# Channel attention and an ELU feed-forward layer on one core: the idle products behind the last real ones

## The chip, the cores and the metric

The kernel runs on one core of a Trainium2 chip. The metric is the device time of one execution in microseconds, given as the median of several runs.

## The reference

Attention over channels, followed by a two-layer network with an ELU between its layers:

```python
# q, k, v: (4, 6080, 256) float32; w_in: (256, 2048), w_out: (2048, 256) float64
qn = q / (np.linalg.norm(q, axis=1, keepdims=True) + 1e-06)
kn = k / (np.linalg.norm(k, axis=1, keepdims=True) + 1e-06)
s = kn.transpose(0, 2, 1) @ qn / tau            # (4, 256, 256)
a = softmax(s)                                  # exp(s - max), over the sum + 1e-9
x = (v @ a).astype(np.float32).reshape(24320, 256)
h = x @ w_in                                    # (24320, 2048)
g = np.where(h > 0.0, h, np.exp(np.minimum(h, 0.0)) - 1.0)
return (g @ w_out).astype(np.float32)
```

## The kernel before

The four batches are taken one after the other. For each, the kernel forms the 256 x 256 matrix of products of k and q ("gram"), makes the softmax of it, and multiplies it into the first weights, so that `v @ a @ w_in` becomes `v @ wp` with a `wp` for each batch. These weights lie in the tiles `wps[b]`, one for each of two halves of the channels (`KT` = 2).

The bulk of the time goes into the feed-forward part. The 6080 tokens of a batch are cut into 12 chunks, eight of 512 tokens and four of 496, 48 chunks in all. For each chunk and each of 16 blocks of 128 hidden features there is one step of the main loop: `h_item` makes the hidden values `ph` with six products (L323 to L325), `elu` and `split_g` make the activations `g` from them on ScalarE and VectorE, and `out_item` multiplies them with `w_out` in six products (L361, L363, L365) into `po`. Every number is split into a high and a low part of type float32r, and three products of parts make one of full width: that is why there are three lines. `out_item` for a step stands three steps (`LAG`) behind its `h_item`. The tile `wo` holds the high and low parts of all of `w_out` as (128 partitions, 16 blocks, 2 parts, 256 columns), in one contiguous piece for each partition.

PSUM has 8 buffers: two for the gram matrices, three (`WB`, tag `w`) that `ph` and other short-lived results take in turn, and three for `po`. The order of instructions on each engine follows the order of the program, with the work of the next batch strewn between the steps. Some other products run as full float32 rather than float32r: the product of the softmax with the first weights of batch 0 (L281) and batch 0's gram matrix (L446). L166 is a gram product of the later batches, whose moving operand is two blocks of 256 columns.

The end of the kernel: after the last `out_item` the function `store` copies the last two blocks of `po` to SBUF (L387, L381, L382) and stores them (L389, L383 from SyncE's queue, L384 from ScalarE's). Behind the main loop, at the end of the program, stand twelve more products on TensorE whose result, the tile `pd`, nobody reads (L696 to L702):

- three (L696) with weights from `wp` and a moving operand of 496 columns from `vt`, the last chunk of v;
- three (L698) with the moving operand replaced by one column repeated 496 times, and weights from `wo`, `wp`, `wo`;
- three (L700) with both operands read as bfloat16;
- three (L702) with only 64 of the 128 rows.

All twelve write into one `pd`, a buffer of the ring of three.

Of the kernel before, what the change touches and what calls it, by code (L numbers as in the profile page):

```python
# [7 lines left out]
F32 = mybir.dt.float32  # L8
F32R = mybir.dt.float32r
U32 = mybir.dt.uint32  # L10
BF16 = mybir.dt.bfloat16
AF = mybir.ActivationFunctionType
ALU = mybir.AluOpType
AX = mybir.AxisListType
# [15 lines left out]
def channel_attention_then_elu_ffn(ctx: ExitStack, tc, q, k, vT, tau, w_in, w_out, outT):  # L30
# [8 lines left out]
    nc = tc.nc  # L39
    B, N, C = q.shape  # L40
# [3 lines left out]
    P = 128  # L44
    KT = C // P
    FT = F // P
    DT = D // P
    CH = 512
    sizes = chunk_sizes(N, CH)
    NB = len(sizes)  # L50
    NCH = B * NB
# [7 lines left out]
    WB = 3  # L59
# [9 lines left out]
    ps = ctx.enter_context(tc.tile_pool(name="ps", bufs=4, space=bass.MemoryType.PSUM))  # L69
# [9 lines left out]
    wo = const.tile([P, FT, 2, D], F32R, name="wo")  # L79
# [213 lines left out]
    def span(c):  # L293

        b, x = divmod(c, NB)
        return b, b * N + sum(sizes[:x]), sizes[x]
# [17 lines left out]
    wps = {}  # L314
# [126 lines left out]
    wi64, wo64, vraw, vts = {}, {}, {}, {}  # L441
# [156 lines left out]
    for c in range(NCH - 1):  # L598
# [6 lines left out]
        x, y = ((1, 2), (4, 6), (17, 19))[c] if c < M - 1 else (c * FT + 9, c * FT + 12)  # L605
# [6 lines left out]
    for b in range(1, B):  # L612
# [31 lines left out]
        for g in range(g0, NG):  # L644
            x = s0 + length * (g - g0) // (NG - g0)
# [5 lines left out]
        x = s1 - FT - 6  # L651
# [12 lines left out]
    for i in range(len(steps) + LAG):  # L664
        if i < len(steps):
            c, f = steps[i]
# [5 lines left out]
        if j >= 0:  # L672
            c, f = steps[j]
# [14 lines left out]

    c, n = NCH - 1, span(NCH - 1)[2]
    pd = ps.tile([P, CH], F32, tag="w", bufs=WB, name="pd")
    hi, lo = (vts[c][:, 0, x, 0:n] for x in range(2))
    wide, narrow = wps[B - 1][0][:, 0, 0:P], wo[:, 0, 0, 0:P]
    for _ in range(3):
        nc.tensor.matmul(pd[:, 0:n], wide, hi, start=True, stop=True)  # L696
    for w in (narrow, wide, narrow):
        nc.tensor.matmul(pd[:, 0:n], w, vts[c][:, 0, 0, 0:1].to_broadcast([P, n]), start=True, stop=True)  # L698
    for w, m in ((wide, hi), (narrow, lo), (wide, hi)):
        nc.tensor.matmul(pd[:, 0:n], w.bitcast(BF16)[:, 0:P], m.bitcast(BF16)[:, 0:n], start=True, stop=True)  # L700
    for w, m in ((wide, hi), (narrow, lo), (wide, hi)):
        nc.tensor.matmul(pd[:, 0:n], w[0 : P // 2], m[0 : P // 2], start=True, stop=True)  # L702


# [29 lines left out]
```

## Time and profile before

| | before |
|---|---|
| median of 3 runs | 2291.22 us (2289.93 to 2294.47) |
| profiled execution: time | 2289.16 us |
| profiled execution: span from first to last instruction | 2287.4 us |
| TensorE busy | 2283.2 us (100%), 10244 products |
| VectorE busy | 1533.4 us (67%) |
| ScalarE busy | 1480.7 us (65%) |
| mean granted TensorE clock | 1.000 |

The time of a run is some 1.8 us longer than the span, which counts from the first to the last instruction of the profiled execution. In the rows below, a line of the order of instructions gives the start in us from the span's start, the duration in us, the engine, the line of the kernel, the operation, what it writes and reads, and how many alike follow one another. PE is TensorE's products, PEld its loads of weights, DVE is VectorE, ACT is ScalarE, SP is SyncE; a q behind an engine's name is its queue. Products are pipelined: the duration of one (0.38 us) is longer than the step from one start to the next.

### The profile page before, as it was taken

The page shows a single profiled execution, that of the slowest core. Times are in us where ns is not written, and L with a number is a line of the kernel's source. Part 1 is how long each engine was busy: PE and PEld are TensorE (multiplying, and loading weights), DVE is VectorE, ACT ScalarE, POOL GpSimd, SP SyncE. Part 2 cuts the span into 40 slices and gives each one's busy share as a digit, 9 for nine tenths or more (in the row PEclk, how much of TensorE's full clock was granted, in tenths as well). Part 3 has the DMA queues.
Part 4 walks back from the last instruction along what each step waited for, and adds up shares of the span by engine and source line. Part 5 has one row for each costly group of instructions (what it writes and reads, how often), then busy time and mean ns, then how long its engine had stood idle before and what let it go on. Part 6 is the DMA issues. An engine that isn't in the chain of part 4 may idle for free.

```text
span 2287.4 us, 27142 instructions
## 1 busy us (share of the span) xinstructions
PE 2283.2 (100%) x10244; PEld 1900.3 (83%) x10244; DVE 1533.4 (67%) x2395; ACT 1480.7 (65%) x2425; POOL 3.2 (0%) x11
## 2 busy tenths in 40 slices
PE   9999999999999999999999999999999999999999
PEld 8778888888888888888888888888888888888888
DVE  6995766666666666666666667666666666666665
ACT  5876666666666666666666666666666666666665
POOL 0000000000000000000000000000000000000000
DMA  9220111110201111111111111121102000000000
GB/s 356 83 74 19 61 59 65 55 53 37 65 28 56 47 53 49 55 55 44 37 55 37 46 47 56 47 64 46 47 34 64 20 19 28 28 19 10 19 9 19
DMA packets 61092, 118.15 MB, mean 52 GB/s; under 512 B 6048, under 2 KB 15904, under 8 KB 60960
## 3 DMA queue, kind: packets, MB, share of 16 engines
q1 hardware_dynamic: 60816, 116.29, 15.0%
q8 instruction: 80, 1.31, 0.2%
q14 instruction: 52, 0.43, 0.1%
q10 hardware_dynamic: 144, 0.13, 0.0%
HBM read 89.39 MB, written 27.00 MB: 51 GB/s over the span
## 4 chain that ended last, share of the span: by engine, by line
PE 97%; DMA 1%; DVE 1%; ACT 0%; issue 0%; SPq 0%; DVEq 0%; ACTq 0%
PE ph L323 15%; PE po L365 15%; PE po L361 15%; PE po L363 15%; PE ph L325 15%; PE ph L324 15%; PE gram L166 3%; PE gram L169 1%; DMA room<-in_k_dram 1%; PE pw L281 1%; PE pw L284 0%; PE pw L285 0%; PE pw L283 0%; DVE acc L145 0%; DMA wi<-in_moe_w_in_dram 0%; DMA raw<-in_k_dram 0%
## 5 line engine op out<-in xcount | busy, mean ns | idle before, releaser
L82 ACT CAST g<-e 128x512 fp32r<-128x512 f32 (+1 forms) x768 | 472.4, 615 | 507.6 <-DVE e L340 275.2
L83 DVE TENSOR_TENSOR g<-e,g 128x512 fp32r<-128x512 f32 (+1 forms) x768 | 526.4, 685 | 349.4 <-ACT g L82 314.1
L361 PE MATMUL po<-g,wo 128*128 128x512 f32 (+1 forms) x1536 | 596.0, 388 | 0.3 <-ACT g L82 0.3
L365 PE MATMUL po<-g,wo 128*128 128x512 f32 (+1 forms) x1536 | 596.0, 388 | 0.0
L363 PE MATMUL po<-g,wo 128*128 128x512 f32 (+1 forms) x1536 | 595.4, 388 | 0.0
L323 PE MATMUL ph<-vt,wp 128*128 128x512 f32 (+1 forms) x1472 | 573.6, 390 | 0.0
L325 PE MATMUL ph<-vt,wp 128*128 128x512 f32 (+1 forms) x1472 | 570.7, 388 | 0.0
L324 PE MATMUL ph<-vt,wp 128*128 128x512 f32 (+1 forms) x1472 | 569.6, 387 | 0.0
L336 DVE SCALAR_TENSOR_TENSOR e<-e,ph 128x512 f32<-128x512 f32 (+1 forms) x416 | 283.6, 682 | 297.2 <-ACT e L335 296.4
L334 ACT ACTIVATE e<-ph 128x512 f32<-128x512 f32 (+1 forms) x416 | 247.1, 594 | 159.2 <-PE ph L325 155.7
L361 PEld LDWEIGHTS po<-g,wo 128*128 128x128 f32 x1536 | 288.4, 188 | 58.3 <-ACT g L82 0.7
L363 PEld LDWEIGHTS po<-g,wo 128*128 128x128 f32 x1536 | 288.4, 188 | 57.7
L365 PEld LDWEIGHTS po<-g,wo 128*128 128x128 f32 x1536 | 288.3, 188 | 52.3 <-DVE g L83 0.4
L323 PEld LDWEIGHTS ph<-vt,wp 128*128 128x128 f32 x1472 | 276.2, 188 | 56.6 <-PE po L365 0.6
L325 PEld LDWEIGHTS ph<-vt,wp 128*128 128x128 f32 x1472 | 276.3, 188 | 56.3
L324 PEld LDWEIGHTS ph<-vt,wp 128*128 128x128 f32 x1472 | 276.4, 188 | 56.0 <-issue 0.7
L335 ACT ACTIVATE e<-e 128x512 f32<-128x512 f32 (+1 forms) x416 | 261.2, 628 | 12.1
L338 ACT ACTIVATE e<-ph 128x512 f32<-128x512 f32 (+1 forms) x352 | 208.7, 593 | 79.2 <-PE ph L325 64.7
L340 DVE TENSOR_TENSOR e<-ph,e 128x512 f32<-128x512 f32 (+1 forms) x352 | 241.1, 685 | 10.7
L339 DVE TENSOR_SCALAR e<-e 128x512 f32<-128x512 f32 (+1 forms) x352 | 148.9, 423 | 49.7 <-ACT e L338 49.6
L145 DVE TENSOR_TENSOR acc<-acc,sq 128x1024 f32<-128x1024 f32 x84 | 102.6, 1221 | 12.1 <-ACT sq L144 11.4
L166 PE MATMUL gram<-qk 128*128 128x512 f32 x276 | 108.5, 393 | 0.0
(126 smaller groups left out, 1173.4 us busy)
## 6 DMA issues: line engine op xcount, KB each, us to landing
raw<-in_q_dram SPq DMA_DIRECT2D x73, 256.0 KB, 2.7
raw<-in_k_dram SPq DMA_DIRECT2D x73, 256.0 KB, 2.9
v<-in_v_dram SPq DMA_DIRECT2D x32, 512.0 KB, 3.4
out_dram<-o SPq DMA_DIRECT2D x56, 256.0 KB, 2.0
v<-in_v_dram SPq DMA_DIRECT2D x16, 496.0 KB, 3.5
out_dram<-o SPq DMA_DIRECT2D x31, 248.0 KB, 2.1
wraw<-w_scr SPq DMA_DIRECT2D x12, 512.0 KB, 3.1
room<-in_q_dram SPq DMA_DIRECT2D x16, 256.0 KB, 5.2
```

The costliest lines, as they stand in the source:

```text
L82: nc.scalar.copy(hi, src)
L83: nc.vector.tensor_sub(lo, src, hi.bitcast(F32))
L323: nc.tensor.matmul(ph[:, 0:n], wp[kt][:, 0, fs], hi, start=(kt == 0), stop=False)
L324: nc.tensor.matmul(ph[:, 0:n], wp[kt][:, 0, fs], lo, start=False, stop=False)
L325: nc.tensor.matmul(ph[:, 0:n], wp[kt][:, 1, fs], hi, start=False, stop=(kt == KT - 1))
L334: nc.scalar.activation(ev, pv, AF.Relu, scale=-1.0)
L335: x = nc.scalar.activation(ev, ev, AF.Exp, scale=-1.0)
L336: y = nc.vector.scalar_tensor_tensor(ev, ev, -1.0, pv, op0=ALU.add, op1=ALU.max)
L340: y = nc.vector.tensor_tensor(ev, pv, ev, op=ALU.max)
L361: nc.tensor.matmul(o, wo[:, f, 0, ds], hi, start=first(c, f), stop=False)
L363: nc.tensor.matmul(o, wo[:, f, 1, ds], hi, start=False, stop=False)
L365: nc.tensor.matmul(o, wo[:, f, 0, ds], lo, start=False, stop=last(c, f))
```

## The change

The twelve idle products go, and 39 others take their place, in ten groups. Each has a `pd` tile of its own from the ring of three PSUM buffers. The moving operand now comes from `wo`, seen as one flat row (`flat`) for each partition; `run(first, n)` is a piece of `n` words that starts `first` words into one of four blocks of 1024, a different one for each product of a group. The weights (`some`) are in turn four blocks of 128 columns of the last batch's `wp`. The groups:

1. four products over 512 words in order;
2. four with weights that are one column repeated 128 times;
3. four over 448 words in place of 512;
4. four that start 4 words later;
5. four that start 16 words later;
6. four that start 32 words later;
7. four that take words from the two halves of the piece in alternation (0, 256, 1, 257, ...);
8. four that take blocks of 16 words from the two halves in alternation;
9. four that take all even words and then all odd ones;
10. three over 512 words in order, with weights from `wo`.

```diff
-    c, n = NCH - 1, span(NCH - 1)[2]
-    pd = ps.tile([P, CH], F32, tag="w", bufs=WB, name="pd")
-    hi, lo = (vts[c][:, 0, x, 0:n] for x in range(2))
-    wide, narrow = wps[B - 1][0][:, 0, 0:P], wo[:, 0, 0, 0:P]
-    for _ in range(3):
-        nc.tensor.matmul(pd[:, 0:n], wide, hi, start=True, stop=True)
-    for w in (narrow, wide, narrow):
-        nc.tensor.matmul(pd[:, 0:n], w, vts[c][:, 0, 0, 0:1].to_broadcast([P, n]), start=True, stop=True)
-    for w, m in ((wide, hi), (narrow, lo), (wide, hi)):
-        nc.tensor.matmul(pd[:, 0:n], w.bitcast(BF16)[:, 0:P], m.bitcast(BF16)[:, 0:n], start=True, stop=True)
-    for w, m in ((wide, hi), (narrow, lo), (wide, hi)):
-        nc.tensor.matmul(pd[:, 0:n], w[0 : P // 2], m[0 : P // 2], start=True, stop=True)
+    flat = wo.rearrange("p f x d -> p (f x d)")
+    left = [wps[B - 1][kt][:, 0, x : x + P] for kt in range(KT) for x in (0, P)]
+
+    def probe(count, weights, moving):
+        for x in range(count):
+            pd = ps.tile([P, CH], F32, tag="w", bufs=WB, name="pd")
+            m = moving(x)
+            out = pd[:, 0 : m.free_size()]
+            if len(m.shape) == 3:
+                out = out.rearrange("p (a b) -> p a b", b=m.shape[2])
+            if len(m.shape) == 4:
+                out = out.rearrange("p (a b c) -> p a b c", b=m.shape[2], c=m.shape[3])
+            nc.tensor.matmul(out, weights(x), m, start=True, stop=True)
+
+    def some(x):
+        return left[x % 4]
+
+    def run(first, n=CH):
+        return lambda x: flat[:, x % 4 * 2 * CH + first : x % 4 * 2 * CH + first + n]
+
+    probe(4, some, run(0))
+    probe(4, lambda x: wps[B - 1][0][:, 0, x : x + 1].to_broadcast([P, P]), run(0))
+    probe(4, some, run(0, 448))
+    probe(4, some, run(4))
+    probe(4, some, run(16))
+    probe(4, some, run(32))
+    probe(4, some, lambda x: run(0)(x).rearrange("p (a b) -> p b a", a=2))
+    probe(4, some, lambda x: run(0)(x).rearrange("p (a b c) -> p b a c", a=2, c=16))
+    probe(4, some, lambda x: run(0)(x).rearrange("p (a b) -> p b a", b=2))
+    probe(3, lambda x: flat[:, 4096 + x * P : 4096 + x * P + P], run(0))
```

More of the change, by code (lines that the diff above doesn't have):

```diff
@@ L10 @@
 U32 = mybir.dt.uint32
-BF16 = mybir.dt.bfloat16
 AF = mybir.ActivationFunctionType
```

## The prediction

> **What bounds the kernel now.** I read the page first (span, busy time, chain), then the order of instructions over the last 8 us, then what the end of the program waits for, and last the spacing of products of 512 columns elsewhere in the span. From the page, the span, TensorE's busy time and the chain that ended last:
>
> ```profile
> span 2287.4 us, 27142 instructions
> PE 2283.2 (100%) x10244; PEld 1900.3 (83%) x10244; DVE 1533.4 (67%) x2395; ACT 1480.7 (65%) x2425; POOL 3.2 (0%) x11
> PE 97%; DMA 1%; DVE 1%; ACT 0%; issue 0%; SPq 0%; DVEq 0%; ACTq 0%
> ```
>
> TensorE is busy for all but 4.2 us of the span, and 97% of the chain is its own. So a product that is added behind the last one lengthens the program by its step, start to start, unless something else ends later. What stands there is in the order of instructions of the last stretch (start, duration, engine, line):
>
> ```profile
> 2282.18 0.38 PE L361 MATMUL po<-g,wo 128*128 128x496 f32 x1
> ...
> 2283.04 0.57 ACT L387 COPY o<-po 128x496 f32<-128x496 f32 x1 [2.04 <-PE po L365]
> ...
> 2283.28 0.38 PE L365 MATMUL po<-g,wo 128*128 128x496 f32 x1
> ...
> 2283.50 0.82 PE L696 MATMUL pd<-vt,wp 128*128 128x496 f32 x3
> ...
> 2283.94 0.19 PEld L698 LDWEIGHTS pd<-vt,wo 128*128 128x128 f32 x1
> ...
> 2284.16 0.37 PE L698 MATMUL pd<-vt,wo 128*128 128x496 f32 x1
> ...
> 2284.37 0.38 PE L698 MATMUL pd<-vt,wp 128*128 128x496 f32 x1
> ...
> 2284.55 0.38 ACTq L384 DMA_DIRECT2D out_dram<-o  x1
> 2284.58 0.37 PE L698 MATMUL pd<-vt,wo 128*128 128x496 f32 x1
> ...
> 2285.23 0.37 PE L700 MATMUL pd<-vt,wp 128*128 128x496 bf16 x1
> 2285.53 0.18 PEld L702 LDWEIGHTS pd<-vt,wp 64*128 64x128 f32 x1 [0.41 <-issue]
> 2285.53 0.49 PE L702 MATMUL pd<-vt,wp 64*128 64x496 f32 x1
> ...
> 2286.08 0.39 PE L702 MATMUL pd<-vt,wp 64*128 64x496 f32 x1
> ```
>
> The last real product starts at 2283.28. The twelve idle ones follow without a gap, from 2283.50 to the last start at 2286.08, and that one ends at 2286.47. Beside them run the last copies and the last store of the output (issued at 2284.55). How long the stores take, and what the program's end (SyncE, at the line that closes the kernel) waits for, stand in the answer on the output's DMAs and in SyncE's waits; the chain's last four pieces follow:
>
> ```profile
> DMA to landing us min/median/max: 1.8/1.9/2.0
> SPq L729 <- DMA out_dram<-o: 1.8, 1, 1.8
> SPq L729 <- PEq L729: 0.6, 2, 0.4
> 2283.66 0.66 PE pd L696 x3
> 2284.32 0.63 PE pd L698 x3
> 2284.95 0.64 PE pd L700 x3
> 2285.60 0.87 PE pd L702 x3
> ```
>
> The last store lands at 2284.55 + 1.8 to 2.0 = 2286.35 to 2286.55, the last product ends at 2286.47: the two tie within 0.1 us, and the chain gives the end to the products. From 2286.47 to 2287.4 there are 0.9 us of closing work, which stay as they are. So the idle products cost next to nothing today, since they lie beside the last copies and stores. That cover is used up: each microsecond more of them is a microsecond more of the program. Nothing on the other engines is late.
>
> **The change part by part.** *Removed*: the twelve products, 2286.08 − 2283.50 = 2.58 us from first start to last start. *Added*: 39 products at the same place in program order. 35 have 512 columns and four have 448, all of float32r words, each with its own weight load. Nothing moves on DVE, ACT or a DMA queue; no vector or scalar instruction reads the results, so no wait is added elsewhere.
>
> The step of an ordinary product comes from two stretches. The first is a steady run of 512 columns (24 products between the two rows); the second is one with 496 columns, above. The third pair of rows is of a product whose 512 columns lie in two separate blocks of 256, with the product behind it:
>
> ```profile
> 2084.62 0.39 PE L361 MATMUL po<-g,wo 128*128 128x512 f32 x1
> ...
> 2089.83 0.39 PE L325 MATMUL ph<-vt,wp 128*128 128x512 f32 x1
> ...
> 401.96 0.40 PE L166 MATMUL gram<-qk 128*128 128x512 f32 x1
> 402.19 0.39 PE L361 MATMUL po<-g,wo 128*128 128x512 f32 x1
> ...
> 140.35 1.72 PE pw L281 x4
> ```
>
> Between the first two rows lie 23 steps: 5.21 / 23 = 0.2265 us for 512 columns in order. For 496 it is (2283.28 − 2282.18) / 5 = 0.220. Both are 0.443 ns a column. The product with a jump after 256 columns takes 0.23, so one jump costs nothing visible. The products of L698, whose moving operand is one column repeated 496 times, take 0.21 (2284.16, 2284.37, 2284.58), or 0.42 ns a column. The difference of 0.02 ns is about a twentieth of a column. I read it as the price of walking: roughly one column's time for each 16 columns (64 bytes) that an ordinary walk passes, and none where the walk stays on one word. That is an estimate from these rows, and no row shows a walk that jumps with every column. The upper row for one is L281, the full float32 products, which run as two instructions each: 1.72 / 4 = 0.43 us for 512 columns, double time.
>
> Group by group, in the order of the diff:
> 1. Four in order, 512 columns: 4 × 0.2265 = 0.91.
> 2. Four with one weight column repeated 128 times. The load of weights takes 0.19 (L698's row) beside the product ahead of it, under the step of 0.2265, so I take 0.91. If such a load took double (0.38) it would stick out by 0.15, 0.6 in all; if repeating saves load time, nothing is won, since it is hidden.
> 3. Four of 448 columns: 448 × 0.443 ns = 0.198, together 0.79.
> 4. to 6. Twelve that begin 4, 16 or 32 words later. By the reading above a late start touches at most one stretch more, one column in 512. 12 × 0.2265 = 2.72.
> 7. Four that alternate between two halves 256 words apart, column by column. Bounds: 0.2265 if the walk is free, and 0.86 (a whole L281 product, two instructions) if it is worse than double. I take 0.43, one column's time for each new place, which is also L281's figure for one instruction: 1.72.
> 8. Four that alternate between the halves in blocks of 16 words. The number of 64-byte stretches is that of an ordinary walk, and a jump between blocks cost nothing in L166: 0.91.
> 9. Four that take every second word and then the others. They pass 64 stretches where an ordinary walk passes 32, so 0.0135 us more each: 0.24, together 0.96. The bounds are 0.2265 and 0.43.
> 10. Three in order with weights from the other array: 0.68.
>
> The sum is 0.91 + 0.91 + 0.79 + 2.72 + 1.72 + 0.91 + 0.96 + 0.68 = 9.60 us. Less the last step, the last start lies 9.37 us behind 2283.50, at 2292.87, and it ends 0.39 later as today. The change is 9.37 − 2.58 = +6.8 us. The profiled execution would come to a span of 2294.2 and a time of 2289.16 + 6.8 = 2296.0. The median of the runs shown, 2291.22, lies 2.06 above that execution; on it, 2298.0.
>
> For groups 7 and 9 there is a rule in the Trainium skill, "SBUF — State Buffer", section "SBUF: two separate sides": the memory is read in lines of 16 bytes, two hits on a line are needed to hide its access, and each access that crosses to a new line pays. By it group 7 (one word per line) pays and group 9 (two words per line) does not: 9.54 in place of 9.60. No row here shows either walk.
>
> A further item is where the results go. Each new product writes a tile of its own, in the ring of three PSUM buffers that the real `ph` products used, where the twelve shared one tile. The writer before it in a buffer is again TensorE, three products earlier, and ends 0.39 after its start, while the next user starts 3 × 0.2265 = 0.68 after it. I cost it at nothing.
>
> **The rivals.** *Cheap walks* (the change does little that a walk can feel). If groups 7 and 9 go at 0.2265 like L166's, the sum is 35 × 0.2265 + 0.79 = 8.72, and the change 8.72 − 0.23 − 2.58 = +5.9: 2297.1. If all go at L698's 0.21, 0.42 ns a column, it is about +5.4: 2296.6. For it speaks L166; against it, that L698 shows a walk does have a price.
>
> *Dear walks.* If a column from a new place costs as much as a whole L281 product, group 7 takes 4 × 0.86 = 3.44, and if group 9 takes 0.43, 1.72: the sum rises by 2.48, the change to +9.3, 2300.5. Nothing in the profile speaks for it but the absence of such a row.
>
> *Waits on the ring of buffers.* If each product from the fourth on waits until TensorE has reported the one three earlier, the load of weights starts late. The nearest row for a step whose weight load was not ahead is the change from L700 to L702: 0.30 in place of 0.22, so 36 × 0.08 = 2.9 more: +9.7, 2300.9. Against it: 0.39 is less than 0.68, and real `ph` products go round the same ring at 0.22.
>
> *Placed ahead.* The new operands (`wo`, the last `wp`) are ready long before the end, so the products could be put among the last real ones. TensorE has no idle time there to take them, and then the last copies and stores, 2286.55 − 2283.28 = 3.3 us from the last real start, would follow all 39: last real start 2283.28 + 9.6, landing 3.3 later, against 2286.47 today, +9.7: 2300.9. Against it: the operands of the twelve (`vt`, `wp`, `wo`) were also ready by then, and they ran behind L365.
>
> *Not slower.* The products have no reader. If the build dropped them, the end would belong to the last store at 2286.35 to 2286.55, a change of −0.1 to +0.1: 2291.2. It decides only if none of the 39 is in the trace. Against it: the twelve have no reader either and all twelve are there.
>
> **How the numbers follow.** The difference that a measurement can tell from none is about 0.2%, 4.6 us. The forecast has 0.62, cheap walks 0.22, dear walks 0.07, ring waits 0.04, placed ahead 0.03, dropped 0.02. All but the last are over 4.6 us. But the three runs shown lie between 1.3 below their median and 3.3 above it, and medians of two kernels can differ by 1 to 2 us: I give one in ten of the forecast (6.8, a margin of 2.2) and a quarter of the cheap walks (a margin of 0.8 to 1.3) to a difference within 0.2%: 0.06 + 0.06, and with the dropped case about 0.13. Faster by over 0.2% has no mechanism; 0.02 for what I have not thought of. Slower is 0.85. The range goes from cheap walks less the runs' spread, 2296.6 − 2.1 = 2294.5, to the dear ones with some spread, 2301.5.
>
> **What would show it right or wrong.** The real products should end as today, the last L365 starting near 2283.3, and DVE and ACT should have the same instruction counts. TensorE's count should rise by 27 to 10271. In the tail, groups 1, 2, 4 to 6, 8 and 10 should step at 0.2265, group 3 at 0.198, group 9 near 0.24 and group 7 near 0.43; the last product should end 6.8 us later, the last store landing where it does now, and SyncE's last wait should be for TensorE alone. It is wrong if the 39 stand ahead of the last L365, if a wait appears within them, if group 7 steps at 0.23 or at over 0.5, or if the stretch before 2283 changes length.

## The result and the profile after

| | before | after |
|---|---|---|
| median | 2292.26 us (2289.93 to 2294.47, 5 runs) | 2298.68 us (2297.58 to 2302.35, 5 runs) |
| profiled execution: time, span | 2289.16, 2287.4 us | 2298.68, 2296.9 us |
| last real product starts | 2283.28 us | 2285.86 us |
| first to last start of the idle products | 2.58 us (12) | 9.54 us (39) |

The ratio of after to before is 1.003, with a 95% interval of 1.0016 to 1.0045. The kernel became slower by 6.4 us at the medians, 0.28%. The page of after, its span, busy times and chain:

```profile
span 2296.9 us, 27196 instructions
PE 2291.4 (100%) x10271; PEld 1907.1 (83%) x10271; DVE 1533.3 (67%) x2395; ACT 1479.8 (64%) x2425; POOL 3.1 (0%) x11
PE 97%; DMA 1%; DVE 1%; ACT 0%; issue 0%; SPq 0%; ACTq 0%; DVEq 0%
```

TensorE has 27 products more; VectorE and ScalarE have the same counts. The order of instructions at the end of after, and then what SyncE waited for there (the lines of the kernel are one lower than before, L364 is L365):

```profile
2285.86 0.38 PE L364 MATMUL po<-g,wo 128*128 128x496 f32 x1
...
2286.08 9.23 PE L702 MATMUL pd<-wo,wp 128*128 128x512 f32 x36
...
2287.13 0.37 ACTq L383 DMA_DIRECT2D out_dram<-o  x1
...
2295.14 0.88 PE L702 MATMUL pd<-wo 128*128 128x512 f32 x3
```
```profile
SPq L746 <- PE pd L702: 7.0, 1, 7.0
SPq L746 <- DMA out_dram<-o: 1.8, 1, 1.8
```

All 39 idle products stand behind the last real one, without a gap. The last store is issued at 2287.13 and waited for 1.8 us; after that SyncE waits another 7.0 us for TensorE alone. Before, the two ended within 0.1 us of each other.

The span grew by 9.5 us, more than the tail: 6.95 us (9.535 − 2.583, unrounded) are the idle products, and 2.6 us were lost before the last real product. Busy time in two stretches of the start (length, then TensorE's busy time and products, weight loads, DVE, ACT, POOL, granted clock, DMA), first of before, then of after:

```profile
40.00:50.00 10.00, 9.40 (x48) 8.05 (x47) 8.11 (x11) 6.03 (x8) 0.00 (x0) 1.00 1.05 410
50.00:60.00 10.00, 9.90 (x48) 8.34 (x47) 7.84 (x23) 4.63 (x13) 0.00 (x0) 1.00 0.45 176
```
```profile
40.00:50.00 10.00, 7.45 (x38) 6.30 (x37) 9.01 (x10) 5.83 (x7) 0.00 (x0) 1.00 1.04 402
50.00:60.00 10.00, 10.00 (x44) 8.54 (x44) 5.93 (x21) 3.99 (x11) 0.00 (x0) 0.83 0.63 244
```

The idle time is one wait of TensorE, for VectorE's sum of the squares of the first batch (again before, then after):

```profile
PE pn L185 <- DVE acc L182: 0.6, 1, 0.6
```
```profile
PE pn L184 <- DVE acc L181: 2.5, 1, 2.5
```

After, TensorE idles 2.55 us where before it idled 0.60, and then it has a granted clock of 0.83 on average over 10 us. All this is in the first batch, 2.2 ms ahead of the change. Every other kernel profiled has the long wait, 2.3 to 3.2 us, and the one execution of before is alone with 0.6. The start varies between executions: the last real product starts at 2284.27 in a kernel with no idle products at all (below), and between 2285.16 and 2288.59 in five others that differ only in their tails. So the medians, and the tails by themselves, carry the comparison, not the two profiled spans.

The steps by group follow, as stretches from the first start of each group to the first start of the next, TensorE alone (length, busy time, products that lie at least in part in the stretch, clock, DMA); the last is that of two steps:

```profile
2286.08:2286.99 0.91, 0.91 (x5) 1.00 0.00 0
2286.99:2287.92 0.93, 0.93 (x5) 1.00 0.94 351
2287.92:2288.73 0.81, 0.81 (x5) 1.00 0.68 224
2288.73:2289.66 0.93, 0.93 (x5) 1.00 0.00 0
2289.66:2290.59 0.93, 0.93 (x5) 1.00 0.00 0
2290.59:2291.51 0.92, 0.92 (x5) 1.00 0.00 0
2291.51:2292.38 0.86, 0.86 (x5) 1.00 0.00 0
2292.38:2293.34 0.97, 0.97 (x5) 1.00 0.00 0
2293.34:2295.14 1.79, 1.79 (x5) 1.00 0.00 0
2295.14:2295.62 0.48, 0.48 (x3) 1.00 0.00 0
```

Group 7, alternation between two halves, is the cheapest of those with 512 columns: 0.86 / 4 = 0.215 us a step, less than a walk in order. Group 9, every second word, is the dearest: 0.45.

### The profile page after: what moved, and what is told of

It reads as the page before. It is cut to its first block, busy times and chain, and to the rows that moved or that the text cites. A ratio compares the mean times of both kernels' runs of the same rounds, so it can differ in the third digit from the quotient of the medians.

```text
span 2296.9 us, 27196 instructions
## 1 busy us (share of the span) xinstructions
PE 2291.4 (100%) x10271; PEld 1907.1 (83%) x10271; DVE 1533.3 (67%) x2395; ACT 1479.8 (64%) x2425; POOL 3.1 (0%) x11
## 4 chain that ended last, share of the span: by engine, by line
PE 97%; DMA 1%; DVE 1%; ACT 0%; issue 0%; SPq 0%; ACTq 0%; DVEq 0%
PE po L364 15%; PE ph L322 15%; PE po L362 15%; PE po L360 15%; PE ph L324 15%; PE ph L323 15%; PE gram L165 3%; PE gram L168 1%; DMA room<-in_k_dram 1%; PE pw L280 1%; PE pw L284 0%; PE pw L282 0%; PE pw L283 0%; DVE acc L144 0%; PE pd L702 0%; DMA raw<-in_k_dram 0%
## 5 line engine op out<-in xcount | busy, mean ns | idle before, releaser
L364 PE MATMUL po<-g,wo 128*128 128x512 f32 (+1 forms) x1536 | 596.0, 388 | 0.0
L364 PEld LDWEIGHTS po<-g,wo 128*128 128x128 f32 x1536 | 288.3, 188 | 52.1 <-DVE g L82 0.3
```

The costliest lines, as they stand in the source:

```text
L364: nc.tensor.matmul(o, wo[:, f, 0, ds], lo, start=False, stop=last(c, f))
```

## The experiments

**No idle products.** The tail is left out (from `flat = ...` to the last `probe`).

> Leaves out all idle products. Theory (the tail is serial behind the last real product, and today's twelve lie beside the last stores): the end goes to the last store, which lands 3.1 to 3.3 us after the last real start; against the kernel before a change of -0.1 to +0.1 us, ratio 1.000, and against the changed kernel about -7 us. Rival (the idle products matter beyond their own time, for instance by where the program's instructions lie, so that the first 60 us differ): the stretch ahead of the last real product changes by 2 us or more in every run.

Measured: 2292.02 us against 2292.38 for the kernel before on the same chip, ratio 1.0001 (0.9992 to 1.001). SyncE's waits at its end:

```profile
SPq L712 <- DMA out_dram<-o: 1.8, 1, 1.8
SPq L712 <- PEq L712: 0.6, 2, 0.4
```

The end belongs to the last store. From the last real start to the end of the span it is 4.02 us (2288.29 − 2284.27), before it was 4.08 (2287.36 − 2283.28). The twelve were free, as their cover said. The start also shows the long wait in this kernel (2.6 us, here with a granted clock of 1.00 behind it), with no idle products, so that wait isn't the work of the 39. The rival, a stretch ahead of the last real product that changes by 2 us or more, is not borne out: it changed by 1.0 us, and the medians with and without the twelve lie 0.4 us apart.

**Twice the 39.**

```diff
+    (the ten probe lines once more)
```

> Issues the 39 products twice, 78 in all. Theory (serial, nothing absorbed): the tail from first to last start is 9.54 us longer plus one step, 19.3 us in all, and the time is about 16.7 us over the kernel before (ratio 1.0073). Each of the ten groups steps the second time as it did the first, within 3%. Rival (part of the tail's cost belongs to the place, to the copies and stores beside its first products or to the ring of buffers filling): the second set of 39 is faster or slower than the first by 0.5 us or more.

Measured: 2308.52 us, 16.1 over the kernel before; ratio 1.0073 (1.0061 to 1.0086). The two sets, stretches from the first start to the first start of the second set, and from there to the last start:

```profile
2287.72:2297.49 9.77, 9.77 (x40) 1.00 0.14 52
2297.49:2307.00 9.51, 9.51 (x39) 1.00 0.00 0
```

The second lacks its last step (0.23), so the sets agree within 0.03 us. Nothing is absorbed, and the copies and stores beside the first set cost it nothing.

**Walks in isolation.** A walk is the order in which the columns of the moving operand are read; two streams are two runs of words that a walk takes in alternation. This kernel and the three that follow replace the 39 products by others. Each ran once, so their steps are compared within one execution. The first:

```diff
-    (the ten probe lines)
+    def every(s): return lambda x: flat[:, 0 : s * CH].rearrange("p (b a) -> p a b", a=s)[:, x % s]
+    def streams(a, n=CH): return lambda x: run(0, n)(x).rearrange("p (a b) -> p b a", a=a)
+    def apart(d): return lambda x: flat[:, x * 1024 : x * 1024 + 2 * d].rearrange("p (a b) -> p b a", a=2)[:, 0:256]
+    def blocks(c): return lambda x: run(0)(x).rearrange("p (a b c) -> p b a c", a=2, c=c)
+    (groups of four with these)
```

> Replaces the 39 products by 25 groups of four, each with another walk of the moving operand. In order: 0.2265 to 0.235. Theory L (lines of 16 bytes, one of them per four column times, and a few kept open): every 2nd word 0.45, every 3rd 0.64 to 0.68, every 4th 0.86 to 0.90, every 8th the same as every 4th; two and four interleaved streams 0.2155, eight and sixteen slower; distance 512 or 260 like 256. Theory B (banks taken by the lowest bits of the word's number): every 3rd word 0.22 to 0.23 since odd steps meet no conflict, every 4th 0.88, every 8th 1.7; the distance of 260 differs from 256. Theory C (words come in pairs of 8 bytes): every 2nd, 3rd, 4th and 8th word all 0.45. The 16-word blocks of the changed kernel stepped at 0.242: by L smaller blocks of 2, 4 and 8 words go at 0.2155 to 0.24 as well. If a late start costs by itself, starts 4, 16 and 32 words later step at 0.230 to 0.236 here too; if it was their place in the tail, at 0.2265. Weights taken from every 2nd word: hidden (no change), unless the load gets longer than a step: then 0.3 or more.

The stretches of every 2nd, 3rd, 4th and 8th word, then of two, four, eight and sixteen interleaved streams, then of blocks of 2 words:

```profile
2286.29:2288.08 1.79, 1.79 (x5) 1.00 0.79 284
2288.08:2289.87 1.80, 1.80 (x5) 1.00 0.00 0
2289.87:2291.72 1.84, 1.84 (x5) 1.00 0.00 0
2291.72:2293.44 1.73, 1.73 (x5) 1.00 0.00 0
...
2298.09:2298.95 0.86, 0.86 (x5) 1.00 0.00 0
2298.95:2300.08 1.12, 1.12 (x5) 1.00 0.00 0
2300.08:2302.10 2.03, 2.03 (x5) 1.00 0.00 0
2302.10:2303.84 1.74, 1.74 (x5) 1.00 0.00 0
...
2307.32:2308.62 1.30, 1.30 (x5) 1.00 0.00 0
```

Every step over one word costs the same, 0.43 to 0.46 us, be it 2, 3, 4 or 8. Theory L asked for 0.64 and 0.86 at 3 and 4, B for 0.22 at 3: both fall. C holds for the steps. But two streams are free (0.215, also at distances of 512, 260 and, for 496 columns, 248 words), four cost 0.28, eight 0.51, and blocks of two words 0.33, which C doesn't explain. Blocks of 4, 8 and 16 words go at 0.25, 0.245 and 0.24. Weights taken from every second word did not change the steps.

**All in order, one buffer.**

```diff
-    (the ten probe lines, a pd for each product)
+    pd = ps.tile([P, CH], F32, tag="w", bufs=WB, name="pd")
+    for x in range(39):
+        nc.tensor.matmul(pd, some(x), run(0)(x), start=True, stop=True)
```

> 39 products of 512 columns, all in order as in group 1, all into one PSUM buffer instead of the ring of three. Theory (the ring costs nothing, the walks make the difference): steps of 0.2265 to 0.23, first to last start 8.6 to 8.75 us where the changed kernel has 9.54. Rival (the ring of buffers or the place in the tail gave the 0.23 to 0.236 of groups 2 to 6): all steps 0.2265 with one buffer (the ring), or steps rising to 0.23 and more from the sixth product on (the place).

Measured: 8.61 us from first to last start, every step 0.225 to 0.228; one run, 2297.07 us. That is 0.92 us less than the 9.54, although four of the changed kernel's products are shorter than any here: this much the other walks cost, with the small extra of groups 2 to 6. It also looked as if the ring gave the 0.23 of groups 2 to 6; the next kernel says otherwise.

**Ring, and two readings of the walks.**

```diff
-    (the ten probe lines)
+    (12 in order, a buffer each; 12 in one buffer; 12 with a new buffer every three)
+    def near(d): return lambda x: run(0)(x).rearrange("p (k a b) -> p k b a", a=2, b=d)
+    def far(s): return lambda x: flat[:, 0 : s * CH].rearrange("p (a b s) -> p s b a", a=2, s=s)[:, x % s]
+    (groups of four with these, each in one buffer)
```

> Replaces the 39 products by groups that tell two readings of the walks apart, and the cost of the ring of buffers. Jitter: twelve in order with a buffer each from the ring, twelve in one buffer, twelve with a change of buffer every three. If a change of buffer costs, the first and third set step at 0.229 to 0.236 after the first few and the second at 0.2265; starts 4 and 32 words later and repeated weights, in one buffer, then step at 0.2265 too. If it is the offsets or weights themselves: 0.230 to 0.236 there. Walks, reading D (two words are taken at a time, and they must lie in the same 8 bytes or far apart): alternation at a distance of 2 to 32 words 0.43 to 0.50, at 128 words about 0.28 or less, and two streams 256 s words apart, each by steps of 2, 3, 4 or 8 words, 0.2155, although no neighbour of any word is ever used. Reading E (a fetched pair of words is held until its second word is used): alternation at 2 to 128 words 0.2155, and the stepped pairs of streams 0.43 to 0.46, as one stepped stream has.

All 36 products in order stepped at 0.225 to 0.228, whatever the buffers: the ring costs nothing. The groups behind them, starts 4 and 32 words later and repeated weights, took 0.224 to 0.239 in one buffer, and a group in order at the very end, behind every 8th word, took 0.231 to 0.254. Once the kind of product had changed, steps in order stayed some 0.005 higher on average. Why is open; it is 0.2 us in the changed kernel. The stretches of alternation at a distance of 2 and of 4 words, then of two far streams by steps of 2, 3, 4 and 8 words:

```profile
2299.75:2300.68 0.93, 0.93 (x5) 1.00 0.00 0
2300.68:2301.54 0.86, 0.86 (x5) 1.00 0.00 0
...
2305.86:2306.78 0.93, 0.93 (x5) 1.00 0.00 0
2306.78:2308.13 1.34, 1.34 (x5) 1.00 0.00 0
2308.13:2309.93 1.80, 1.80 (x5) 1.00 0.00 0
2309.93:2311.77 1.85, 1.85 (x5) 1.00 0.00 0
```

D falls with near alternation (0.215 at 4 words), E with the far streams by 2 (0.23). What fits is a count per stream: with two streams the price follows how many words each takes from a 16-byte line (four: 0.215, two: 0.23, one and a third: 0.34, one: 0.45). With the far streams the price rises from steps of 2 to 4 words (0.23, 0.34, 0.45) and hardly further at 8 (0.46), as it would where four words make a line.

**The reading tested.** If TensorE takes even and odd columns as two streams, a walk in order gives each stream two words of a line (words 0 and 2, 1 and 3), and every second word gives it one. Three walks tell it from pairs of 8 bytes.

```diff
-    (the ten probe lines)
+    def doubled(x): return run(0, 256)(x).unsqueeze(2).to_broadcast([P, 256, 2])
+    def parts(n, s): return lambda x: flat[:, 0 : CH // n * s].rearrange("p (b s) -> p b s", s=s)[:, :, 0:n]
+    (groups of four with these, and alternations by steps of 2 and 4 words)
```

> Replaces the 39 products by ten groups of four, to test a reading of the earlier walks: TensorE takes the odd-numbered and the even-numbered columns as two streams, and each stream is free with four words from a 16-byte line in a row, costs some 6% with two and double with one. Groups: in order; each of 256 words twice (0, 0, 1, 1, ...); two words of every four; two words of every eight; four of every eight; four of every sixteen; the words 0, 8, 2, 10, 4, 12, 6, 14 and so on; the words 0, 16, 4, 20 and so on; two halves in alternation; in order. Reading P (streams by the parity of the column): 0.2265 to 0.235; 0.2155; 0.45; 0.45; 0.23 to 0.25; 0.23 to 0.25; 0.23; 0.45 to 0.46; 0.2155; 0.23. Reading E (words come in pairs of 8 bytes, one pair in two column times, whatever the column's number): 0.2265; 0.2155; 0.2265 to 0.24; the same; the same; the same; 0.45; 0.45; 0.2155; 0.23. They part at the third, fourth and seventh group.

The stretches of the second to the eighth group:

```profile
2287.72:2288.59 0.86, 0.86 (x5) 1.00 0.92 348
2288.59:2290.38 1.79, 1.79 (x5) 1.00 0.34 116
2290.38:2292.23 1.85, 1.85 (x5) 1.00 0.00 0
2292.23:2293.18 0.95, 0.95 (x5) 1.00 0.00 0
2293.18:2294.09 0.91, 0.91 (x5) 1.00 0.00 0
2294.09:2294.96 0.88, 0.88 (x5) 1.00 0.00 0
2294.96:2296.83 1.87, 1.87 (x5) 1.00 0.00 0
```

0.215, 0.45, 0.46, 0.24, 0.23, 0.22 and 0.47: reading P holds where the two part (0.45 for two words of four and of eight, where E asked for 0.23; 0.22 for the seventh group, where E asked for 0.45). Its misses here are small, 0.22 for 0.23 and 0.47 for 0.45 to 0.46. Three earlier walks it doesn't fit: with four streams, eight streams or blocks of two words each stream of columns changes its line with every word, which should cost 0.45, and they took 0.28, 0.51 and 0.33. So it is a reading that forecast this kernel's groups, not a mechanism that the runs show in full.

**A version that beats both.** If order costs two column streams some 5%, the real products pay it too. Here all products of the feed-forward part read their moving operand as group 7 does; the copies behind the second product put the tokens back. Of the lines below, the one with `vt` is in `h_item`, the one with `g` in `out_item` and the last in `store`, where the four quarters of the tokens are put back in order.

```diff
+    def halves(t):
+        return t.rearrange("p (a b) -> p b a", a=2)
...
+            hi, lo = (halves(vt[:, kt, x, 0:n]) for x in range(2))
...
+        hi, lo = (halves(g[:, x, 0:n]) for x in range(2))
...
+                nc.scalar.copy(in_quarters(o[:, dt, 0:n]), in_place(po[dt][:, 0:n]))
...
```

> All 9024 real products of the feed-forward part take their moving operand from its two halves in alternation, as group 7 did (0.2155 and, for 496 columns, 0.209, where in order it is 0.2265 and 0.220); the order of the tokens that this gives is undone in the copies that follow the second product. No idle products. If the gain holds beside busy vector and scalar engines: 9024 x 0.011 = 99 us less, some 2193 us, ratio 0.957. Rival (the extra of an ordinary walk is hidden by something else in the loop, a wait on ScalarE or VectorE or the loads of weights, or the alternation collides with their reads): a gain of less than a third of that, with steps of 0.22 and more in the main loop or waits of TensorE for g.

Measured: 2190.29 us (2188.32 to 2191.64, 5 runs) against 2293.02, ratio 0.9552 (0.9539 to 0.9565): 102.7 us less, where 99 were expected. The kernel has 9216 such products; the 9024 leave out 192 that read from a tile of another name (`scr_r`). With all of them the working gives 9216 × 0.011 = 101 us. Busy times of its page, two products of 512 columns 28 steps apart, and busy time in a stretch where both kernels have 512 columns (order of engines as above), of this kernel and last of the kernel before:

```profile
PE 2177.1 (99%) x10232; PEld 1910.5 (87%) x10232; DVE 1517.8 (69%) x2395; ACT 1466.7 (67%) x2425; POOL 3.1 (0%) x11
```
```profile
1899.78 0.38 PE L334 MATMUL ph<-vt,wp 128*128 128x512 f32 x1
...
1905.82 0.38 PE L335 MATMUL ph<-vt,wp 128*128 128x512 f32 x1
```
```profile
1885.00:1905.00 20.00, 20.00 (x95) 17.50 (x94) 12.36 (x21) 13.08 (x22) 0.00 (x0) 1.00 0.08 26
```
```profile
1885.00:1905.00 20.00, 20.00 (x90) 16.57 (x89) 11.85 (x19) 12.54 (x21) 0.00 (x0) 1.00 0.16 53
```

The step is 6.04 / 28 = 0.2157 where it was 0.2265. In the same 20 us the kernel before had 90 products of 512 columns, this one 95; VectorE and ScalarE still have a third of the time to spare, so the rival of a hidden wait falls. The copies that put the tokens back are no dearer (587 ns for 512 columns, before 588).

## Why the prediction was right or wrong

- *The products are serial and the cover is used up*: right. The last product ends 7 us behind the stores, SyncE's last wait is for TensorE, and doubling the set adds its whole length.
- *Twelve products cost next to nothing*: right; without them the ratio is 1.0001.
- *The time*: forecast 2298.0, measured 2298.68; the change forecast +6.8, measured +6.95 in the tails and +6.4 at the medians. The forecast's direction and size were right, but the sum was right by luck, since its two uncertain terms were both wrong (next point). Two of the prediction's own signs of being wrong came: group 7 stepped at 0.215, and the stretch before 2283 changed length.
- *Group 7*: wrong. Forecast 1.72 us, measured 0.86 (lower bound 0.2265 a step, measured 0.215): a jump with every column is free where each second column goes on at the word behind its last. *Group 9*: wrong the other way. Forecast 0.96, measured 1.79 (upper bound 0.43 a step, measured 0.45). The two errors, −0.86 and +0.83, cancel. The step that failed is the reading of the price of walking, one column's time for each new 64-byte stretch: the steps of 2 to 8 words all cost the same, and two streams cost nothing.
- *The rule for groups 7 and 9*: the Trainium skill, "SBUF — State Buffer", section "SBUF: two separate sides", wants two hits on a 16-byte line. As I applied it, to the whole walk, it put the price on group 7 and none on group 9; the trace shows the opposite (0.215 and 0.45 a step). Counted for even and odd columns apart it agrees with most of the runs: two words of a line in each of the two streams cost 0.23, one costs 0.45; four streams (0.28) and blocks of two words (0.33) it still misses. That its sum, 9.54, equals the measured 9.54 is chance: the sum has the last step in it and the measured stretch has not.
- *Groups 1, 3, 10*: 0.91, 0.81 and some 0.71 for 0.91, 0.79 and 0.68. *Groups 2, 4 to 6 and 8*: 0.93, 2.78 and 0.97 for 0.91, 2.72 and 0.91; the weights and late starts aren't the cause (the same extra appears in order, after other products), and this small part is open.
- *Cheap walks* came true for group 7 alone. *Dear walks* had group 9 nearly right (1.72, measured 1.79) and group 7 four times too dear (3.44, measured 0.86). *Waits on the ring* fell: products in order step at 0.2265 with a buffer each. *Placed ahead* and *not slower* fell: all 39 stand behind the last L364.
- *The stretch before the last real product would not change*: it did, by 2.6 us in the profiled executions, from the start of the kernel. It is the wait for VectorE and the clock behind it, and the kernel with no idle products has that wait too. The start varies in kernels with any tail, so I take it as no effect of the change; what sets it was not tried.

## What to carry to other kernels

Here work behind the last real product was free up to the moment when the last store landed, and cost its full length from there. Try reading a float32r moving operand as two streams in alternation, one for even and one for odd columns, each contiguous: here that took 5% off each large product and 4.5% off a kernel that TensorE bounds. A single walk by steps of 2, 3, 4 or 8 words doubled the product. And a sum that comes out right can hide two wrong terms: look at each group before trusting the price list.

## What the runs showed of the hardware that was not expected

- A moving operand in order is not the fastest: 0.2265 us for 512 columns, 0.2155 when it alternates between two pieces 4 to 512 words apart (16 to 2048 bytes).
- The number of streams matters: one 0.2265, two 0.2155, four 0.28, eight 0.51, sixteen 0.435. That eight are dearer than sixteen, and that four cost so little, fits no reading given here.
- Words repeated twice in a row (0, 0, 1, 1, ...) go at 0.2155 too.
